# One array shape for all products but the scores: a retention layer with its feed-forward block on one core

## The chip, the cores and the metric

The kernel runs on one core of a Trainium2 chip. The metric is the device time of one execution in microseconds. The core has a TensorE (PE in the profile, its weight loads PEld), a VectorE (DVE), a ScalarE (ACT), a GpSimd (POOL) and a SyncE (SP), which here only issues DMAs. Matmuls write to PSUM; the other engines copy from there to SBUF.

## The reference, cut to what matters

```python
# q, k, v: (8 batches, 8 heads, 576 tokens, 64) float32
scores = matmul(q, k.transpose(0, 1, 3, 2)) / sqrt(64)
gamma = 1.0 - 2.0 ** (-5.0 - arange(8))                  # one decay per head
Dmat = where(rel >= 0, gamma[:, None, None] ** rel, 0.0)  # rel = query pos - key pos
attn = matmul(scores * Dmat, v)
x = attn.transpose(0, 2, 1, 3).reshape(4608, 512)
h = x @ w_in                                              # (4608, 1024)
solu = h * softmax(h)
ln = (solu - mean(solu)) / sqrt(var(solu) + 1e-6) * g_ln
out = ln @ w_out                                          # (4608, 512) float32
```

## The kernel before, in words

The 4608 tokens are taken in 36 chunks of 128. Batches go in pairs: of each pair, four chunks of 128 tokens of each batch in turn (c = 0 to 3), and then one chunk that holds the last 64 tokens of both (c = 4), four such chunks in all. The decay is taken apart into a factor on the query, one on the key or value and a state that is carried from chunk to chunk, so that inside a chunk only a triangular mask (tris) is needed. In the two-batch chunks the first 64 partitions hold one batch and the last 64 the other, and the second mask of tris cuts them apart.

Each step of a chunk is a short function with a two-letter name, and the order of all steps on all engines is written out by hand in three strings: START, LOOP (run once a chunk for 21 chunks in the middle) and END. An engine does its instructions in that order. LOOP is

```python
LOOP = """
tr:2 so:-1 tu:-2 ld:6 er:2:v m1:0 dk:0 kv:1 eu:-2:a kd:4 ad:1 cv:3:g av:1 mx:0 sc:2 sq:-2 fs:1
ex:1:a rt:-2 cq:4:g xp:0 m2:-2 d3:0 ck:5:g st:-2 mk:2
"""
```

where the number is the chunk, counted from the one in hand, and a letter names the engine (a ScalarE, v VectorE, g GpSimd). The steps that matter here:

- ld loads q, k and v of a chunk from SP's queue (L185, L192); a two-batch chunk takes two DMAs of 64 partitions for each. st scales a result on ScalarE and stores it (L523, L528).
- cq, ck and cv scale q and v (L210, L199) and cast k (L171) to 16 bits, mostly on GpSimd.
- tr and tq transpose q (and k, where a DMA does not do it) on TensorE by a product with the identity (tr L256, tp L232); er and eq copy the result to SBUF (qkT, L171).
- sc makes the scores of a head from 64 rows of the array, two heads side by side, one on the upper rows and one on the lower (L290, 64\*128 in the profile); mk masks them on VectorE (ret, L303).
- kv makes the state's new part (kp, L314) and av the masked scores times v (x, L365). Each matmul of these fills 64 columns of the array, and a pair of heads goes side by side (128\*64).
- ad adds the state on VectorE (t, L329, or L327 where a batch begins), dk and d3 scale it on GpSimd (s, L341 and L353), and fs adds the state's share to x (L380, on the whole array, 128\*128).
- ex casts x to xT; m1 is the product with w_in (h, L412; in START also L400, a row of w_in at a time), eight matmuls of 512 columns on the whole array. mx takes the maximum (nm, L422), xp the exponential (e, L428), so multiplies (u, L437).
- tu transposes u (lp, L495; in END du does it by a DMA, L500), eu copies it (uT), and m2 is the product with w_out (o, L515), again eight matmuls of 512 columns on the whole array. sq and rt make the normalisation (L465, L477 to L487).
- In END the last chunk goes in two halves of its columns (hm, hx, hp, ho, ht, he, hq, h2, hw), and hw stores each half with two DMAs, one on SP's and one on ScalarE's queue (L638).
- c1, at the start, sends for the table small (L650) and lets GpSimd make the identity and the masks.

A matmul on the profile is written rows\*columns of the array, then the output's partitions x elements. Each matmul has a weight load of its own ahead of it.

Of the kernel before, what the change touches and what calls it, by code (L numbers as in the profile page):

```python
# [10 lines left out]
FP = mybir.dt.float32  # L11
F16 = mybir.dt.float16
BF16 = mybir.dt.bfloat16
P = 128
# [55 lines left out]
def _np_tables():  # L70


    g = 1.0 - 2.0 ** (-5.0 - np.arange(H, dtype=np.float64))
    p = np.arange(P)
    gq = (g[None, :] ** p[:, None]) / 8.0
    gk = g[None, :] ** (-p[:, None])
    j = np.arange(8)
    gqt = (g[2 * (p[:, None] % 4) + j // 4] ** (4 * (p[:, None] // 4) + j % 4)) / 8.0
    gqm = (g[2 * (p[:, None] % 4) + j // 4] ** ((4 * (p[:, None] // 4) + j % 4) % 64)) / 8.0
    gkt = g[None, :] ** (-(p % 64)[:, None])  # L80


    gs = np.zeros((P, 4))
    gd = np.zeros((P, 4, 2))
    for e in range(2):
        for hp in range(4):
            gs[e * 64 : e * 64 + 64, hp] = g[2 * hp + e] ** 128.0
        gd[e * 64 : e * 64 + 64, :, e] = gs[e * 64 : e * 64 + 64]
    small = np.concatenate([gq, gk, gqt, gkt, gs, gd.reshape(P, 8), gqm], axis=1).astype(np.float32)
    return small  # L90
# [3 lines left out]
def kernel(  # L94
# [10 lines left out]
    nc = tc.nc  # L105
# [28 lines left out]

    def rows(n):

        bs, c = chunks[n]
        if c < 4:
            return [(slice(0, P), bs[0], c * P)]
        return [(slice(64 * i, 64 * i + 64), b, 4 * P) for i, b in enumerate(bs)]  # L140


    small = const.tile([P, 52], FP, name="small")
    tris = const.tile([P, 2, P], FP, name="tris")
# [14 lines left out]
    gd = small[:, 36:44].rearrange("p (a b) -> p a b", a=4)  # L159
    gqm = small[:, 44:52]  # L160

# [10 lines left out]


    def quads(n):

        return n != NCH - 2

    def ld(n):

        for key, src in (("qf", q), ("kf", k), ("vf", v)):  # L180
            dst = load.tile([P, H, D], FP, name=key, bufs=6 if key == "kf" else 7)
            for pp, b, s0 in rows(n):
                m = pp.stop - pp.start
                if key == "qf" and quads(n):
                    nc.sync.dma_start(  # L185
                        out=dst[pp].rearrange("p (h a) d -> p h (a d)", h=2),
                        in_=src[b, :, s0 : s0 + m, :].rearrange(
                            "(g h) (t a) d -> t g h (a d)", h=2, a=4
                        ),
                    )  # L190
                    continue
                nc.sync.dma_start(  # L192
                    out=dst[pp], in_=src[b, :, s0 : s0 + m, :].rearrange("h p d -> p h d")
                )
            T[key, n] = dst

# [29 lines left out]
    def tq(n):  # L226

        tp = bank([P, 2, 4, P], F16, "tp")
        for i, src in enumerate((T.pop(("q16", n)), T["k16", n])):
            s2 = src.rearrange("p h d -> p (h d)")  # L230
            for hp in range(4):
                nc.tensor.transpose(  # L232
                    out=tp[:, i, hp], in_=s2[:, hp * P : (hp + 1) * P], identity=ident
                )
        T["tp", n] = tp
# [14 lines left out]
    def tr(n):  # L250
        if chunks[n][1] == 4 or n < BY_DMA:
            return tq(n)
        tp = bank([P, 4, P], F16, "tr")
        s2 = T.pop(("q16", n)).rearrange("p h d -> p (h d)")
        for hp in range(4):
            nc.tensor.transpose(  # L256
                out=tp[:, hp], in_=s2[:, hp * P : (hp + 1) * P], identity=ident
            )
        T["tp", n] = tp
# [6 lines left out]
    def turned(engine, n, out, tp):  # L266

        if not quads(n):
            return copy(engine, out, tp)
        copy(  # L270
            engine, out.rearrange("p g (t a) -> p g t a", a=4),
            tp.rearrange("p a (t g) -> p g t a", g=4),
        )
# [98 lines left out]
    def fs(n):  # L372

        bs, c = chunks[n]
        qkT = T.pop(("qkT", n))
        s16 = [T.pop(("s16", b, c)) for b in bs] if c > 0 else []
        w = P // len(bs)
        for hp in range(4):
            for i, s in enumerate(s16):
                nc.tensor.matmul(  # L380
                    out=T["x", n][:, hp, i * w : (i + 1) * w],
                    lhsT=s[:, hp].rearrange("p e d -> p (e d)"),
                    rhs=qkT[:, 0, hp, i * w : (i + 1) * w],
                    start=False, stop=i == len(s16) - 1, skip_group_check=True,
                )
        T["xs", n] = T.pop(("x", n))
# [6 lines left out]
    def mr(n, d):  # L393

        d = int(d)
        done = T.get(("rows", n), 0)
        if done == 0:
            T["h", n] = ps_h.tile([P, DFF], FP, tag="h", name="h")
        for i in range(2):
            nc.tensor.matmul(  # L400
                out=T["h", n][:, i * 512 : (i + 1) * 512], lhsT=T["xT", n][:, d],
                rhs=w_in16[:, d, i * 512 : (i + 1) * 512], start=done == 0, stop=done == 3,
            )
        T["rows", n] = done + 1

    def m1(n):

        xT = T.pop(("xT", n))
        h = ps_h.tile([P, DFF], FP, tag="h", name="h")
        for i in range(2):  # L410
            for d in range(4):
                nc.tensor.matmul(  # L412
                    out=h[:, i * 512 : (i + 1) * 512], lhsT=xT[:, d],
                    rhs=w_in16[:, d, i * 512 : (i + 1) * 512], start=d == 0, stop=d == 3,
                )
        T["h", n] = h
# [73 lines left out]
    def tu(n):  # L490

        u = T.pop(("u", n))
        lp = bank([P, NF, P], F16, "lp")
        for c in range(NF):
            nc.tensor.transpose(out=lp[:, c], in_=u[:, c * P : (c + 1) * P], identity=ident)  # L495
        T["lp", n] = lp
# [11 lines left out]
    def m2(n):  # L508

        uT = T.pop(("uT", n))  # L510
        o = bank([P, DM], FP, "o")
        assert T["w_out"] == NF and (n < PLAIN or T["w_cen"] == NF)
        w = w_out16 if n < PLAIN else T["w_c"]
        for c in range(NF):
            nc.tensor.matmul(  # L515
                out=o, lhsT=uT[:, c], rhs=w[:, c], start=c == 0, stop=c == NF - 1
            )
        T["o", n] = o

    def st(n):  # L520

        o_sb = moe.tile([P, DM], FP, name="o_sb", bufs=4)
        nc.scalar.activation(  # L523
            out=o_sb, in_=T.pop(("o", n)), func=ACT.Copy, scale=T.pop(("rs", n))
        )
        for pp, b, s0 in rows(n):
            m = pp.stop - pp.start
            nc.sync.dma_start(out=out[b * S + s0 : b * S + s0 + m, :], in_=o_sb[pp])  # L528


    def hm(n, i):
# [5 lines left out]
        for d in range(4):  # L537
            nc.tensor.matmul(
                out=h, lhsT=T["hx", n][:, d], rhs=w_in16[:, d, i * 512 : (i + 1) * 512],
                start=d == 0, stop=d == 3,  # L540
            )
        T["hh", n, i] = h
# [40 lines left out]
    def ht(n, i):  # L583
# [3 lines left out]
        for c in range(4):  # L587
            nc.tensor.transpose(out=lp[:, c], in_=u[:, c * P : (c + 1) * P], identity=ident)
        T["hlp", n, i] = lp
# [24 lines left out]
    def h2(n, i):  # L614
# [3 lines left out]
        for c in range(NF):  # L618
            nc.tensor.matmul(
                out=o, lhsT=T["huT", n, c // 4][:, c % 4], rhs=T["w_c"][:, c, w], start=c == 0,  # L620
                stop=c == NF - 1,
            )
        T["ho", n, i] = o

    def hw(n, i, e):
# [6 lines left out]
        else:  # L632
            nc.vector.tensor_scalar(
                out=o_sb, in0=o, scalar1=rs, scalar2=None, op0=ALU.mult, op1=ALU.bypass
            )
        for queue, (pp, b, s0) in zip((nc.sync, nc.scalar), rows(n)):
            m = pp.stop - pp.start
            queue.dma_start(out=out[b * S + s0 : b * S + s0 + m, w], in_=o_sb[pp])  # L638


    def wu(_, count):

        w = bank([P, 512], FP, "w")
        for _ in range(int(count)):
            nc.tensor.matmul(
                out=w, lhsT=warm[:, 0:P], rhs=warm, start=True, stop=True, skip_group_check=True
            )

    def c1(_):
# [11 lines left out]
        )  # L661
        nc.gpsimd.memset(tris.rearrange("p a b -> p (a b)"), 1.0)
        nc.gpsimd.affine_select(
            out=tris, in_=tris, pattern=[[0, 2], [1, P]], channel_multiplier=-1, base=0,
            compare_op=ALU.is_ge, fill=0.0,
        )
        nc.gpsimd.affine_select(
            out=tris[:, 1, 64:], in_=tris[:, 1, 64:], pattern=[[0, 64]], channel_multiplier=1,
            base=-64, compare_op=ALU.is_ge, fill=0.0,
        )  # L670
# [45 lines left out]
    def mm(_):  # L716
# [3 lines left out]
        for c in range(NF):  # L720
            nc.tensor.matmul(
                out=T["mean"], lhsT=ones, rhs=w_out16[:, c], start=c == 0, stop=c == NF - 1
            )

# [53 lines left out]
```

## Time and profile before

| | us |
|---|---|
| median of 3 runs | 217.29 (215.56 to 219.33) |
| the profiled execution | 218.18 |
| its span | 216.5 |
| PE busy (matmul records) | 197.4 (91%), 1989 matmuls |
| DVE busy | 180.8 (84%) |
| POOL busy | 173.6 (80%) |
| ACT busy | 167.1 (77%) |
| DMA on SP's queue | 111904 packets, 46.55 MB, 92.7% of 16 engines' span |

The span is the time between the first and the last instruction of the profiled execution, and 1.7 us of its time lie around it. Matmuls overlap in the records: the records of a group of matmuls last longer than the distance between their starts, so a busy share of PE is not a share of its peak. The granted TensorE clock is 0.9 or more of full speed in all 40 slices of the page. DMA shares above 1 occur in single stretches, since packets of one engine overlap too.

### The profile page before, as it was taken

What the parts mean: (1) busy time and instruction counts of PE and PEld (TensorE: products, weight loads), DVE (VectorE), ACT (ScalarE), POOL (GpSimd) and SP (SyncE); (2) the same over time, 40 slices, a digit from 0 to 9 for tenths busy, and PEclk for the clock granted to TensorE, in tenths of its full rate; (3) what the DMA queues carried; (4) which work ended last, traced back from release to release, by engine and by line L of the source; (5) the groups of instructions that cost most, each with busy time, mean ns of one, the idle gap of its engine ahead of it and who ended that gap; (6) DMA issues with size and microseconds to landing.
All of it is one profiled execution on the core that took longest, in us unless ns stands there. A gap on an engine that the chain in (4) does not pass through costs nothing.

```text
span 216.5 us, 5376 instructions
## 1 busy us (share of the span) xinstructions
PE 197.4 (91%) x1989; PEld 110.8 (51%) x1989; DVE 180.8 (84%) x289; ACT 167.1 (77%) x279; POOL 173.6 (80%) x275
## 2 busy tenths in 40 slices
PE   0379889896999999999999999999999999999993
PEld 0254456453455555555555555555555565545451
DVE  1378899999997998888888898888888999889840
ACT  2073988966897888888888788888888794986991
POOL 3348889997367899999997899999997899977340
PEclk9999999999999999999999999999999999999999
DMA  5999999998986899799999998899999999674845
GB/s 137 289 317 287 228 280 358 193 245 224 270 228 168 219 183 201 177 225 258 243 223 232 255 208 186 186 247 248 214 227 213 253 181 190 145 172 100 195 109 182
DMA packets 112250, 47.04 MB, mean 217 GB/s; under 512 B 96984, under 2 KB 106208, under 8 KB 112224
## 3 DMA queue, kind: packets, MB, share of 16 engines
q1 hardware_dynamic: 111904, 46.55, 92.7%
q8 instruction: 15, 0.25, 0.5%
q10 hardware_dynamic: 320, 0.16, 0.3%
q14 instruction: 11, 0.09, 0.2%
HBM read 32.54 MB, written 9.44 MB: 194 GB/s over the span
## 4 chain that ended last, share of the span: by engine, by line
PE 78%; DVE 13%; DMA 2%; issue 2%; SPq 2%; ACT 1%; DVEq 0%; ACTq 0%
PE o L515 26%; PE h L412 23%; PE sc L290 5%; PE lp L495 5%; PE x L365 4%; PE x L380 3%; PE kp L314 3%; DVE nm L422 3%; DVE ret L303 2%; DMA vf<-in_v_dram 2%; PE tp L232 2%; PE tr L256 2%; PE h L400 2%; DVE u L437 2%; DVE q L210 1%
## 5 line engine op out<-in xcount | busy, mean ns | idle before, releaser
L412 PE MATMUL h<-w_in,xT 128*128 128x512 f16 x264 | 62.4, 379 | 0.5 <-DVE u L437 0.5
L515 PE MATMUL o<-w_c,uT 128*128 128x512 f16 x240 | 56.5, 379 | 0.6 <-DVE t L327 0.4
L428 ACT ACTIVATE e<-h,nm 128x1024 f32<-128x1024 f32 x35 | 39.0, 1116 | 14.0 <-DVE nm L422 14.0
L303 DVE TENSOR_TENSOR ret<-sc,tris 128x512 f16<-128x512 f32 x72 | 46.1, 682 | 1.3 <-PE sc L290 1.2
L437 DVE SCALAR_TENSOR_TENSOR u<-h,e 128x1024 f16<-128x1024 f32 x35 | 42.7, 1220 | 2.7 <-ACT e L428 1.4
L422 DVE TENSOR_REDUCE nm<-h 128x1 f32<-128x1024 f32 x35 | 42.5, 1216 | 2.0 <-PE h L412 1.5
L515 PEld LDWEIGHTS <-uT 128*128 128x128 f16 x280 | 26.2, 98 | 27.1 <-issue 0.4
L412 PEld LDWEIGHTS <-xT 128*128 128x128 f16 x264 | 24.2, 98 | 24.4 <-issue 0.5
L341 POOL TENSOR_TENSOR s<-t,small 128x512 f16<-128x512 f32 x32 | 34.2, 1070 | 2.6 <-DVE t L329 2.6
L199 POOL TENSOR_TENSOR v<-vf,small 128x512 f16<-128x512 f32 x32 | 33.6, 1051 | 3.0 <-DMA vf<-in_v_dram 3.0
L465 ACT ACTIVATE sq<-u,su 128x1024 bf16<-128x1024 f16 x30 | 34.8, 1159 | 0.1
L210 POOL TENSOR_TENSOR q<-qf,small 128x512 f16<-128x512 f32 x30 | 31.3, 1044 | 1.8 <-DMA qf<-in_q_dram 1.8
L171 ACT CAST xT<-x 128x512 f16<-128x512 f32 x34 | 19.9, 585 | 11.1 <-PE x L380 10.6
L523 ACT ACTIVATE o_sb<-o,rs 128x512 f32<-128x512 f32 x35 | 23.9, 685 | 4.1 <-POOL rs L487 1.6
L171 ACT COPY uT<-lp 128x1024 f16<-128x1024 f16 x25 | 25.3, 1012 | 0.3 <-PE lp L495 0.2
L487 POOL TENSOR_TENSOR rs<-w,mhalf 128x1 f32<-128x1 f32 x36 | 19.8, 551 | 3.0
L483 POOL TENSOR_SCALAR w<-ss,w 128x1 f32<-128x1 f32 x31 | 8.9, 287 | 15.9 <-ACT sq L465 13.9
L171 POOL CAST k<-kf 128x512 f16<-128x512 f32 x28 | 17.1, 611 | 3.0 <-DMA kf<-in_k_dram 3.0
L171 ACT COPY qkT<-tp 128x512 f16<-128x512 f16 x20 | 10.7, 594 | 10.9 <-PE tp L232 10.9
L495 PE MATMUL lp<-ident,u 128*128 128x128 f16 x224 | 17.0, 219 | 1.3 <-DVE u L453 1.3
L353 POOL TENSOR_TENSOR s<-t,small 128x256 f32<-128x256 f32 x24 | 14.9, 622 | 3.4 <-DVE t L327 2.5
L290 PE MATMUL sc<-qkT 64*128 64x128 f16 x288 | 15.2, 225 | 2.0 <-ACT qkT L171 1.2
(89 smaller groups left out, 262.5 us busy)
## 6 DMA issues: line engine op xcount, KB each, us to landing
qf<-in_q_dram SPq DMA_DIRECT2D x32, 256.0 KB, 4.0
kf<-in_k_dram SPq DMA_DIRECT2D x32, 256.0 KB, 4.4
vf<-in_v_dram SPq DMA_DIRECT2D x32, 256.0 KB, 4.7
out_dram<-o_sb SPq DMA_DIRECT2D x32, 256.0 KB, 2.6
w_in<-in_moe_w_in_dram SPq DMA_DIRECT2D x4, 512.0 KB, 6.1
w_out<-in_moe_w_out_dram SPq DMA_DIRECT2D x4, 512.0 KB, 6.7
qf<-in_q_dram SPq DMA_DIRECT2D x8, 128.0 KB, 3.2
kf<-in_k_dram SPq DMA_DIRECT2D x8, 128.0 KB, 3.8
```

The lines of the kernel that those rows point to most:

```text
L171: (engine.copy if engine is nc.scalar else engine.tensor_copy)(out=out, in_=in_)
L199: engine.tensor_tensor(out=dst, in0=T.pop((key, n)), in1=table.unsqueeze(2).to_broadcast([P, H, D]), op=ALU.mult,)
L210: ENG[e].tensor_tensor(out=dst.rearrange("p (a h) d -> p h a d", h=2), in0=T.pop(("qf", n)).rearrange("p (h a) d -> p h a d", h=2), in1=ta ...
L303: nc.vector.tensor_tensor(out=r, in0=s, in1=m, op=ALU.mult)
L341: nc.gpsimd.tensor_tensor(out=s16, in0=t.unsqueeze(2).to_broadcast([P, 4, 2, D]), in1=gd.unsqueeze(3).to_broadcast([P, 4, 2, D]), op=ALU.mult,
L412: nc.tensor.matmul(out=h[:, i * 512 : (i + 1) * 512], lhsT=xT[:, d], rhs=w_in16[:, d, i * 512 : (i + 1) * 512], start=d == 0, stop=d == 3,)
L422: nc.vector.tensor_reduce(out=nm, in_=T["h", n], axis=AX.X, op=ALU.max, negate=True)
L428: nc.scalar.activation(out=e, in_=T["h", n], func=ACT.Exp, bias=T.pop(("nm", n)), accum_out=s)
L437: nc.vector.scalar_tensor_tensor(out=u, in0=T.pop(("h", n)), scalar=-1.0, in1=T.pop(("e", n)), op0=ALU.mult, op1=ALU.mult, accum_out=su,)
L465: nc.scalar.activation(out=s, in_=T.pop(("v", n)), func=ACT.Square, scale=-float(DFF), bias=T.pop(("su", n)), accum_out=ss,)
L495: nc.tensor.transpose(out=lp[:, c], in_=u[:, c * P : (c + 1) * P], identity=ident)
L515: nc.tensor.matmul(out=o, lhsT=uT[:, c], rhs=w[:, c], start=c == 0, stop=c == NF - 1)
```

## The change

All products and transposes on the whole array become two matmuls, each on 64 columns of the array, that write the lower and the upper 64 partitions of the same output (product and turn). Those that were on 64 columns (kv, av) or on 64 rows (sc) stay. The order of the steps and the PSUM banks stay too.

The two-batch chunks hold the two batches' tokens in turn (partition 2t is token t of the first, 2t + 1 of the second), and are loaded with one DMA for each of q, k and v, and stored with one. For that the tables of decays of these chunks, the second mask, the copy of the transposed q and the reads of fs are laid out anew. GpSimd makes the second mask as a product of the first with par, two new columns of small.

```diff
+    def tokens(src, n):
+        bs, c = chunks[n]
+        if c < 4:
+            return src[bs[0], :, c * P : (c + 1) * P, :].rearrange("h t d -> t h d")
+        return src[bs[0] : bs[1] + 1, :, 4 * P :, :].rearrange("b h t d -> t b h d")
...
+    HALF = (slice(0, 64), slice(64, P))
+    def turn(out, in_):
+        for w in HALF:
+            nc.tensor.transpose(out=out[w], in_=in_[:, w], identity=ident)
+    def product(out, lhsT, rhs, start, stop):
+        for w in HALF:
+            nc.tensor.matmul(
+                out=out[w], lhsT=lhsT[:, w], rhs=rhs, start=start, stop=stop,
+                skip_group_check=True,
+            )
...
@@ ld @@
-            for pp, b, s0 in rows(n):
-                m = pp.stop - pp.start
...
+                nc.sync.dma_start(out=dst, in_=tokens(src, n))
...
@@ tq, tr, tu, ht @@
-                nc.tensor.transpose(
-                    out=tp[:, i, hp], in_=s2[:, hp * P : (hp + 1) * P], identity=ident
-                )
+                turn(tp[:, i, hp], s2[:, hp * P : (hp + 1) * P])
...
@@ turned, two-batch chunks @@
+            engine, out.rearrange("p g (t a b) -> p g t a b", a=4, b=2),
+            tp.rearrange("p a (t b g) -> p g t a b", b=2, g=4),
...
@@ fs @@
+        def part(t, i):
+            return t if len(bs) == 1 else t.rearrange("p (t b) -> p b t", b=2)[:, i]
         for hp in range(4):
             for i, s in enumerate(s16):
-                nc.tensor.matmul(
-                    out=T["x", n][:, hp, i * w : (i + 1) * w],
-                    lhsT=s[:, hp].rearrange("p e d -> p (e d)"),
-                    rhs=qkT[:, 0, hp, i * w : (i + 1) * w],
-                    start=False, stop=i == len(s16) - 1, skip_group_check=True,
+                product(
+                    part(T["x", n][:, hp], i), s[:, hp].rearrange("p e d -> p (e d)"),
+                    part(qkT[:, 0, hp], i), False, i == len(s16) - 1,
                 )
...
@@ m1; mr, m2, hm, h2, mm and wu likewise @@
-                nc.tensor.matmul(
-                    out=h[:, i * 512 : (i + 1) * 512], lhsT=xT[:, d],
-                    rhs=w_in16[:, d, i * 512 : (i + 1) * 512], start=d == 0, stop=d == 3,
-                )
+                w = slice(i * 512, (i + 1) * 512)
+                product(h[:, w], xT[:, d], w_in16[:, d, w], d == 0, d == 3)
...
@@ st, two-batch chunks @@
+            nc.sync.dma_start(
+                out=dst[:, 4 * P :, :].rearrange("b t m -> t b m"), in_=o_sb
+            )
...
@@ c1 @@
-        nc.gpsimd.affine_select(
-            out=tris[:, 1, 64:], in_=tris[:, 1, 64:], pattern=[[0, 64]], channel_multiplier=1,
-            base=-64, compare_op=ALU.is_ge, fill=0.0,
+        m = tris[:, 1].rearrange("p (t b) -> p t b", b=2)
+        nc.gpsimd.tensor_tensor(
+            out=m, in0=tris[:, 0].rearrange("p (t b) -> p t b", b=2),
+            in1=par.unsqueeze(1).to_broadcast([P, 64, 2]), op=ALU.mult,
         )
```

TensorE has 3145 matmuls after the change and 1989 before it; the instructions of the other engines stay the same in number and order, but for SP's DMAs of the two-batch chunks (three for a load and one for a store, before six and two) and GpSimd's masks in c1.

## The prediction

> **What bounds the kernel now.** I read the page first: the shares of the engines, then the chain that ended last.
>
> ```profile
> span 216.5 us, 5376 instructions
> PE 197.4 (91%) x1989; PEld 110.8 (51%) x1989; DVE 180.8 (84%) x289; ACT 167.1 (77%) x279; POOL 173.6 (80%) x275
> ...
> PE 78%; DVE 13%; DMA 2%; issue 2%; SPq 2%; ACT 1%; DVEq 0%; ACTq 0%
> ```
>
> TensorE is 91% busy and makes up 78% of the chain. The table by stretches of 10 us shows it all but gapless from 60 to 210 us (9.6 to 10.0 busy), while three of the four stretches from 20 to 60 hold only 8.1 to 8.8. So what counts is how closely its groups follow each other. The timeline of PE alone shows that for one round of LOOP; columns are start, time to the end of the last, and the instructions.
>
> ```profile
> 102.33 0.39 PE L232 MATMUL tp<-ident,k 128*128 128x128 f16 x4
> 102.55 0.61 PE L495 MATMUL lp<-ident,u 128*128 128x128 f16 x8
> 103.00 1.89 PE L412 MATMUL h<-w_in,xT 128*128 128x512 f16 x8
> 104.82 0.32 PE L314 MATMUL kp<-v,k 128*64 128x64 f16 x8
> 104.96 0.39 PE L365 MATMUL x<-ret,v 128*64 128x128 f16 x8
> 105.29 0.40 PE L290 MATMUL sc<-qkT 64*128 64x128 f16 x8
> 105.62 0.40 PE L380 MATMUL x<-qkT,s 128*128 128x128 f16 x4
> 105.85 0.38 PE L515 MATMUL o<-w_c,uT 128*128 128x512 f16 x1
> ```
>
> Read starts, not durations, since matmuls overlap. Eight lp matmuls of 128 columns take 102.55 to 103.00, 56 ns each. Eight h matmuls of 512 columns start 216 ns apart, so the next group could start at 104.73; it starts at 104.82. The single records say it exactly: 309 ns from the last h matmul to the first kp, where 216 stand between h matmuls: 93 ns are lost. The same loss stands at x L365 to sc (about 96) and sc to x L380 (92), and none stands at tp to lp, lp to h or L380 to o. What the three places share is a change in the part of the array used: 128\*128, 128\*64 (a column half), 64\*128 (a row half). Over the trace I find 119 such changes between these three shapes; where nothing else is late, each costs 92 to 96 ns. The pair after the first is late too: 52 ns after kp's first instead of 31.
>
> The list of waits shows the same from the side of the weight loads:
>
> ```profile
> PEld L314 <- issue: 9.1, 22, 0.6
> ...
> PEld L365 <- issue: 2.9, 8, 0.4
> PEld L290 <- issue: 2.9, 7, 0.4
> ```
>
> Loads otherwise run ahead of the matmuls; at these lines, the first of a new shape, they sit idle for about 0.4 us and wait for nothing that the profile names.
>
> **The change, part by part.** *Shapes.* turn and product split every matmul on the whole array into two on its column halves. The whole-array shape is then gone (but for gT), and only changes to and from sc are left: 22 from column to row, 13 from whole to row, 32 and 3 back stay as 35 pairs of changes; 34 from whole to column and 15 back vanish, 49 in all. From 57 to 168 us there are 23 of the 49, none with a wait in it: 23 x 93 ns = 2.1 us, and the late second pair, 23 x 21 ns = 0.5 us. After 168 us there are 10 without a wait, 1.1 us with their second pairs; PE waits there now and then for ACT and DVE, so I take 0.7. Before 57 us there are 10, 1.2 us; PE waits there for loads and casts, and I take 0.5. Against it, the pair after the first is 11 ns late when sc gives way to the whole array and 21 ns when h gives way to a column half: 35 x 10 ns = 0.4 us lost. Sum 3.4 us.
>
> *Twice the matmuls.* 580 of 512 columns, 16 of 256, 432 transposes and 128 of x L380 become 1156 more, with as many loads. A pair costs nothing if its halves run side by side. The rows for that are x L365 and kp, which are such pairs already: the halves start 3 to 4 ns apart, and pairs start 56 ns apart at 128 columns and 28 to 29 at 64, as one whole-array matmul would. For 512 columns with one moving operand for both halves no row exists. Bounds: 0 from x L365; above, the one burst where the halves were 16 to 19 ns apart (sc at 185.97 us), 580 x 17 = 9.9 us if it added to every pair. I take 0, as the 56 ns row repeats in every chunk and moves as many columns per ns.
>
> The row of the loads is x L365 again: two loads of 64 columns begin 3 ns apart, and the pair still takes 56 ns. The Trainium skill (TensorEngine Tiling (Array Packing), Restrictions and Gotchas) says that column tiling goes without fast weight load, and (TensorE: Matmul & The Clock Gate, LDWEIGHTS (loading the stationary operand)) that an ordinary load takes its columns over 1.2 ns. As an estimate from these pages, two loads one after the other would be 107 ns, and 432 transposes would lose 51 ns each, 22 us; by that rule the change is a plain loss (a rival below). The trace speaks against it: x L365 lives without the fast load at 56 ns per pair.
>
> *Issue.* A chunk of LOOP has 56 matmuls and 56 loads now (tr 4, tu 8, m1 8, kv, av, sc 8 each, fs 4, m2 8), and 88 of each after: 176 instructions in 5.25 - 0.11 = 5.14 us, 29 ns each. The trace shows 47 ns sustained (5.25 us / 112), which is no limit found, and one burst that is: at 185.86 us PE's sequencer stands in an event wait before sc, and the 16 instructions behind it begin between 185.95 and 186.15, 13 ns each. I take 13, so 0.
>
> *Two-batch chunks.* Four of 36 chunks: loads go from six DMAs of 128 KB to three of 256, stores from two to one (the last chunk keeps two each for its halves). Bytes and pieces stay.
>
> ```profile
> qf<-in_q_dram SPq DMA_DIRECT2D x32, 256.0 KB, 4.0
> kf<-in_k_dram SPq DMA_DIRECT2D x32, 256.0 KB, 4.4
> ...
> kf<-in_k_dram SPq DMA_DIRECT2D x8, 128.0 KB, 3.8
> ```
>
> One large landing at 4.4 us replaces two small at 3.8, issued 0.6 apart: the same time. SP saves three issues of 0.6 us per chunk, which nobody waits for, as loads come one to three chunks ahead. Copies of q and x L380 take elements in steps of two for these chunks; DVE stands idle some 0.5 us a chunk before t L329, which hides 0.1 or 0.2 us, and 8 pairs of 29 ns in each of four chunks could at worst double on PE, 0.9 us. I take 0.1. POOL's new product in tris needs small, which landed 1.6 us after its issue at 0.80; POOL then has 2.71 us of idle time before k L171: 0.
>
> *What follows PE.* A faster PE must be fed. POOL repeats its round of LOOP in 5.39 us while PE needs 5.25:
>
> ```profile
> 87.71 1.04 POOL L341 TENSOR_TENSOR s<-t,small 128x512 f16<-128x512 f32 x1
> ...
> 93.10 1.04 POOL L341 TENSOR_TENSOR s<-t,small 128x512 f16<-128x512 f32 x1
> ...
> 98.50 1.04 POOL L341 TENSOR_TENSOR s<-t,small 128x512 f16<-128x512 f32 x1
> ```
>
> Its s (dk) is what x L380 waits for. In the trace s is ready 1.17 us ahead at the start of such a stretch (chunk at 76.5 us) and 0.61 ahead at 97.5; then come chunks with less for POOL, and the lead returns. With 0.11 us less per chunk the smallest lead is about 0.61 - 5 x 0.11 = 0.05, in the second stretch 0.69 - 0.55 = 0.14. It just holds; I take 0.1 us for it.
>
> Sum: -3.4 + 0.1 + 0.1 = -3.2 us. The profiled execution took 218.18 us (span 216.5 and 1.7 around it), which makes 215.0. The median of the runs shown is 217.29, 0.9 below it; from there, 214.1. I say 214.0.
>
> **The rivals.** *All of it counts:* the waits in the first 57 and last 45 us follow PE, since PE's own results end them. Then the sum is 2.6 + 1.1 + 1.2 - 0.4 = 4.5 us, 212.8. For it: DVE and ACT there wait for tp, x and h. Against: DMA and POOL do too.
>
> *POOL takes the place of the shape changes:* its lead runs out and PE falls into POOL's 5.39 us. For it, the falling lead above; against, POOL's idle time of 14.7 us between 60 and 180. If the lead is gone halfway, half of the loop's 2.6 us goes: 215.4; if all is lost, 217.
>
> *Slower, issue becomes the bound:* 176 instructions a chunk decide as soon as one takes over 29 ns on the average. The nearest sustained row: after the event wait at 109.93 us, 32 instructions up to 110.96 at 30.5 ns each, at the array's own pace there. If that is the limit, a chunk takes 5.37 us, 0.12 more than now, over 30 chunks 3.6 us: 220.9. Against it, the 13 ns burst. The Trainium skill (TensorE: Matmul & The Clock Gate, Step-by-step: what each phase is for) knows a case of about 62 ns per matmul; 88 of them would be 5.46 us a chunk and 6 us more in all. kp's eight matmuls start within 0.12 us, so the trace does not show that, though a queue filled ahead could hide it.
>
> *Slower, pairs of 512 columns do not overlap fully:* from 6 ns per pair (3.4 us / 580) the gain is gone; at 17 ns it is 217.3 - 3.2 + 9.9 = 224.0. The loads belong here too: if the halves of a transposed pair went one after the other, at 56 ns each, 432 x 56 ns = 24 us would come on top, against the row of x L365; of the 0.07 below I give that 0.02.
>
> *The change does not do what it says:* the 93 ns belong to the tensors, not the shape. Against it, groups of one shape but other tensors (tp to lp, lp to h, x L380 to o) follow at the array's own pace. 217.
>
> **How the numbers follow.** My forecast 0.62, all of it counts 0.12, POOL 0.08, no effect 0.03, issue 0.08, pairs 0.07. The runs of before spread over 215.56 to 219.33, so my own case reaches from 211.6 to 216.4. The range 211.0 to 219.5 takes it, the two rivals without effect and the near edge of the slower ones. Faster by over 2% (below 212.9; 2% is about what a measurement of this kernel can tell from no change): a third of my case and two thirds of the next, 0.30. Slower by over 2%: both slower rivals and a rest, 0.17. Within: 0.53.
>
> **What would show it.** Right: kp starts 216 ns after the last pair of h, the PEld waits on issue at kp gone, h pairs 216 ns apart, a LOOP round near 5.14 us, waits of x L380 on POOL under 0.5 us in all. Wrong: pairs of h over 222 ns apart, gaps inside lp or x after an event wait, or PE idle in front of x L380 or sc.

## The result, and the profile after

The first measurement gave 216.35 us median for the changed kernel (214.59 to 221.44, 21 runs) beside 218.08 for the kernel before (215.56 to 219.44, 21 runs): a ratio of 0.9928, with a 95% interval of 0.9899 to 0.9958. The same kernel was measured twice more: 217.96 beside 218.09 (ratio 1.0052, 1.0004 to 1.0099) and 218.43 beside 218.82 (1.0004, 0.9958 to 1.0050). Over all 41 runs of the changed kernel the median is 217.97 us, over the 73 of before in the same three measurements 218.29. So the forecast's sign and range (211.0 to 219.5) stood in the first measurement, at half the forecast gain of 3.2 us, and the repeats leave 0.3 us, which is no difference that these runs can tell from none. The intervals of the first two measurements do not meet, so from one measurement to the next more differs than an interval shows; what it is stays open. (The ratios leave disturbed runs out; the medians take all runs.)

The page of the first profile after, engines and chain:

```profile
span 214.6 us, 7661 instructions
PE 194.8 (91%) x3145; PEld 127.9 (60%) x3145; DVE 178.2 (83%) x289; ACT 166.6 (78%) x279; POOL 173.6 (81%) x275
...
PE 45%; POOL 16%; DMA 13%; DVE 10%; SPq 5%; ACT 5%; issue 4%; POOLq 0%; DVEq 0%; ACTq 0%
```

TensorE's share of the chain falls from 78% to 45%; POOL, DMA and SP's queue come in. TensorE's own groups follow as forecast. Their timeline for a round of LOOP (start, time to the end of the last, instructions):

```profile
78.69 1.68 PE L196 MATMUL h<-w_in,xT 128*64 128x512 f16 x14
80.20 0.29 PE L335 MATMUL kp<-v,k 128*64 128x64 f16 x8
80.32 0.39 PE L386 MATMUL x<-ret,v 128*64 128x128 f16 x8
80.65 0.40 PE L311 MATMUL sc<-qkT 64*128 64x128 f16 x8
80.98 0.41 PE L196 MATMUL x<-qkT,s 128*64 128x128 f16 x8
81.22 1.89 PE L196 MATMUL o<-w_c,uT 128*64 128x512 f16 x16
```

The seven pairs of h shown take 78.69 to 80.20, 216 ns each, and kp follows the last pair at that distance, where it took 309 ns before. The halves of a pair start 3 to 4 ns apart, 128-column pairs 56 ns apart. h starts at 78.47, 83.62, 88.77 and 93.91 us: a round of 5.14 to 5.15, against 5.25. Between the three shapes 70 changes are left of 119, all to or from sc. In the list of the weight loads' waits, kp's line (L335 now) falls from 9.1 us, 22 times, to one wait; the lines of sc and of the pairs' transposes keep 3.3 and 2.4 us:

```profile
PEld L335 <- issue: 0.9, 1, 0.9
```

The loads of the two-batch chunks are single ones now. The k transposes land later than before, in the median 4.9 us after their issue (end of the line) and not 4.2:

```profile
qkT<-k SPq DMA_TRANSPOSE x21, 4.9
```

One group is slower by the change. In the two-batch chunks the matmuls of x L380 (L196 now) read q and write x in steps of two. Before, with the new layout alone (an experiment below) and after, the groups of chunk 17:

```profile
110.75 0.41 PE L380 MATMUL x<-qkT,s 128*128 128x64 f16 x8
```

```profile
111.04 0.62 PE L196 MATMUL x<-qkT,s 128*128 128x64 f16 x8
```

```profile
106.81 0.64 PE L196 MATMUL x<-qkT,s 128*64 128x64 f16 x16
```

The next group starts 0.24, 0.43 and 0.44 us after these. The single records say why: the matmuls of 64 columns start 29 ns apart before, 56 with the steps of two. That is 0.2 us in each two-batch chunk, 0.9 us in the four of the first profile (the last, in END, takes 0.51 beside 0.23).

What became of the change is seen when the same groups are found in four profiles (start in us, and distance to the kernel before):

| TensorE group | before | after, 1st | after, 2nd | after, 3rd |
|---|---|---|---|---|
| tp, early in LOOP | 65.15 | 62.16 (-2.99) | 63.37 (-1.78) | 65.56 (+0.41) |
| sc of chunk 23 | 136.78 | 132.19 (-4.59) | 133.40 (-3.38) | 135.59 (-1.19) |
| sc of chunk 30 | 172.16 | 167.80 (-4.36) | 171.58 (-0.58) | 173.41 (+1.25) |
| lph, near the end | 206.95 | 205.14 (-1.81) | 209.12 (+2.17) | 210.24 (+3.29) |
| span | 216.5 | 214.6 | 218.6 | 219.7 |

From the first row to the second every profile of the changed kernel gains the same 1.6 us: fourteen rounds of 0.11 us (the change of shapes) and a wait of 0.4 us for t at 121.58 us that only the kernel before has there, less what chunk 17 takes more. Ahead of it START decides, anywhere from 3 us early to 0.4 late. Behind it all three lose: 2.8, 5.6 and 4.5 us between the second row and the fourth. The first profile's execution took 216.31 us, near the median of its measurement; the second's and third's took 220.30 and 221.38 us, 2.3 and 3.0 above the medians of theirs, so they show what a large loss is made of, not its usual size. The lists of TensorE's waits from 57 us on (total, times, longest), before, then after in the first and in the third profile:

```profile
PE o L515 <- DVE t L327: 0.4, 1, 0.4
PE tr L256 <- DVE qkT L171: 0.2, 1, 0.2
```

```profile
PE tr L191 <- ACT o_sb L539: 0.9, 1, 0.9
PE o L196 <- DMA uT<-u: 0.6, 1, 0.6
PE x L196 <- POOL s L362: 0.5, 1, 0.5
PE sc L311 <- DVE qkT L183: 0.5, 1, 0.5
PE sc L311 <- DMA qkT<-k: 0.4, 1, 0.4
...
```

```profile
PE sc L311 <- DMA qkT<-k: 2.7, 2, 1.4
PE tr L191 <- ACT o_sb L539: 0.9, 1, 0.9
PE x L196 <- POOL s L362: 0.4, 1, 0.4
...
```

The scores now wait for the k that a DMA transposes: 0.4 us in the first profile, 3.0 in the second, 2.7 in the third. In the first profile, of the first measurement, four other waits are longer.

### The profile page after: what moved, and what is told of

Read it like the earlier page. It is cut to its first block, busy times and chain, and to the rows that moved or that the text cites. A ratio compares the mean times of both kernels' runs of the same rounds, so it can differ in the third digit from the quotient of the medians.

```text
span 214.6 us, 7661 instructions
## 1 busy us (share of the span) xinstructions
PE 194.8 (91%) x3145; PEld 127.9 (60%) x3145; DVE 178.2 (83%) x289; ACT 166.6 (78%) x279; POOL 173.6 (81%) x275
## 4 chain that ended last, share of the span: by engine, by line
PE 45%; POOL 16%; DMA 13%; DVE 10%; SPq 5%; ACT 5%; issue 4%; POOLq 0%; DVEq 0%; ACTq 0%
PE o L196 16%; PE h L196 15%; DMA kf<-in_k_dram 4%; POOL s L362 3%; PE lp L191 3%; POOL v L219 3%; DMA vf<-in_v_dram 3%; DMA qkT<-k 3%; PE sc L311 2%; PE x L196 2%; DMA qf<-in_q_dram 2%; DMA uT<-u 2%; DVE nm L440 2%; SPq L210 2%; POOL q L230 2%
## 5 line engine op out<-in xcount | busy, mean ns | idle before, releaser
L196 PE MATMUL h<-w_in,xT 128*64 128x512 f16 x560 | 67.4, 381 | 0.5 <-DVE w_in L183 0.3
L196 PE MATMUL o<-w_c,uT 128*64 128x512 f16 x480 | 57.2, 380 | 0.8 <-DMA uT<-u 0.6
L196 PEld LDWEIGHTS <-xT 128*64 128x64 f16 x576 | 32.7, 110 | 21.9 <-issue 1.0
L196 PEld LDWEIGHTS <-uT 128*64 128x64 f16 x560 | 32.4, 110 | 22.3 <-DMA uT<-u 1.1
L183 ACT CAST xT<-x 128x512 f16<-128x512 f32 x34 | 19.9, 586 | 10.3 <-PE x L196 10.0
L501 POOL TENSOR_SCALAR w<-ss,w 128x1 f32<-128x1 f32 x31 | 8.3, 267 | 13.3 <-ACT sq L483 11.1
L191 PEld LDWEIGHTS <-q 128*64 128x64 f16 x280 | 12.5, 114 | 9.0 <-issue 2.4
L191 PE MATMUL lp<-ident,u 128*64 128x128 f16 x448 | 17.1, 219 | 0.6 <-DVE u L471 0.6
```

What stands on the lines that cost most here:

```text
L183: (engine.copy if engine is nc.scalar else engine.tensor_copy)(out=out, in_=in_)
L191: nc.tensor.transpose(out=out[w], in_=in_[:, w], identity=ident)
L196: nc.tensor.matmul(out=out[w], lhsT=lhsT[:, w], rhs=rhs, start=start, stop=stop, skip_group_check=True,)
```

## The experiments

**Which half of the change does what.** Pairs alone, in the old layout with six loads and two stores for a two-batch chunk (run twice):

```diff
 kernel before, and:
+    HALF = (slice(0, 64), slice(64, P))
+    def turn ...  def product ...      (as in the change, at all the same places)
```

> The kernel before with all whole-array products and transposes as column pairs, and the two-batch chunks as they were (two DMAs of 64 partitions each). Theory A (the gain is the shape changes, and the last 50 us give part of it back because the last loads and transposes by DMA do not come sooner): the same as the whole change, ratio to before 0.993 (0.990 to 0.996). Rival B (the new layout with one DMA of 256 KB a load is what costs at the end, 4.96 us landing of the last q): without it the gain is whole, 0.985 to 0.988.

> The pairs without the new layout, once more, for a trace at the full clock. Theory A (the pairs gain in the middle, and the end, fed by DMA through SP's queue, gives it back): a round of the middle at 5.14 us as in the whole change, and the excess of 4 to 5 us over the whole change stands after 160 us, where the last two-batch chunk's six loads and two stores hold up the transposes behind them on SP. Rival E (pairs with the old layout lose in the middle, by a mechanism of the array): a round over 5.25 us.

Layout alone, which is the changed kernel with whole-array products:

```diff
-    HALF = (slice(0, 64), slice(64, P))
+    HALF = (slice(0, P),)
```

> The changed kernel with whole-array products and transposes again, so the new layout of the two-batch chunks alone. Theory A: 1.000 (0.997 to 1.003), a round of the middle 5.25 us as before. Rival B: 1.004 to 1.008, slower by the time the last loads land later. Rival C (the fewer DMAs are what gained, the pairs nothing): 0.993.

Pairs alone are slower: ratio to before 1.0156 (1.0095 to 1.0216), again 1.0162 (1.0057 to 1.0266). Layout alone: 1.0036 (1.0000 to 1.0072). Neither half gains, and together they come out better than pairs alone by 1.0 to 2.3%. So an edit that I had put at 0.1 us decides whether the other one costs time. The loss of layout alone is about what x L380 takes more in four chunks (0.19 us each, 0.35% in all). Pairs alone met none of the cases: the round is 5.14 us, but the losses begin before 160 us, with a wait of 1.6 us at 141.46. The waits of pairs alone (second run) say where:

```profile
PE sc L301 <- DMA qkT<-k: 3.3, 3, 1.6
PE x L184 <- POOL s L352: 1.3, 1, 1.3
```

**Is a change of shape worth what I said?** The changed kernel with tu's transposes on the whole array, two more changes in a chunk that has them:

```diff
-            turn(lp[:, c], u[:, c * P : (c + 1) * P])
+            nc.tensor.transpose(out=lp[:, c], in_=u[:, c * P : (c + 1) * P], identity=ident)
```

> The changed kernel with the transposes of u (tu, 28 of 36 chunks) on the whole array again: two changes of shape more in each of 28 chunks. Theory A: each costs 93 ns and up to 20 for the second pair, so a round of the middle takes 5.14 + 0.2 = 5.35 us and the 21 rounds 4 us more; the ratio to before is 1.005 to 1.015. If the changes of shape are not what costs, 0.993 and 5.14 us.

1.0071 (1.0017 to 1.0125). Over 20 rounds (57 to 163 us) TensorE fell 4.14 us behind the first profile after: 0.21 a round, 0.10 per change. The price holds. But from there to the end this kernel got 2.9 us back, as its waits after 57 us were down to this one:

```profile
PE tr L191 <- DVE qkT L183: 0.2, 1, 0.2
```

The slower TensorE meets no other waits there; the faster one runs into the pace of what feeds it. (The ratio alone would hardly show the price: the changed kernel's own three measurements reach from 0.9928 to 1.0052.)

**Does the end hang on SP's queue?** In both kernels, one load in END moved forward in SP's order:

```diff
-... ld:-1 ad:-6 ...   ... d3:-6 ld:0 mx:-6 ...
+... ld:-1 ld:0 ad:-6 ...   ... d3:-6 mx:-6 ...
```

> The changed kernel with the load of the last chunk issued straight behind that of the chunk before it, ahead of two DMA transposes in SP's order (buffers are free by then). Theory A, if the last q and k are late because they are issued late: q of the last chunk lands 3 us sooner, the end gives 1 to 2 us, 0.985 to 0.989. Rival D (the DMA engines are full, 98% of the span, and what is issued sooner only pushes others back): 0.993, with transposes landing later instead.

> The kernel before with the same early load. Theory A: TensorE is the chain there to the end, so 1.000 (0.998 to 1.002). If it gains as much as in the changed kernel (0.993 or less), the late load was a loss of both kernels and not what took the change's gain.

The changed kernel: 1.0081 (1.0034 to 1.0128), with sc waiting 2.5 us for k. The kernel before: 1.0021 (0.9981 to 1.0061), with 0.2 us. Nothing is gained. Of the 2.5 us, 1.6 come at chunk 30, whose transpose is issued ahead of the moved load, and 0.9 at chunk 33, whose transpose stands behind it in SP's queue.

**Are the DMA engines full?** Both kernels store only 128 of 512 columns of the chunks from 20 on (c < 4); the other columns of those outputs are not written:

```diff
-            nc.sync.dma_start(out=dst[0, c * P : (c + 1) * P, :], in_=o_sb)
+            w = slice(0, 128 if n >= 20 else DM)
+            nc.sync.dma_start(out=dst[0, c * P : (c + 1) * P, w], in_=o_sb[:, w])
```

> The changed kernel, where chunks from 20 on store 128 of 512 columns (the rest of their output is left out; two-batch chunks store all), 192 KB less of about 1.2 MB by DMA per chunk. Theory A with full DMA engines: transposes and last loads land sooner, TensorE's waits after 160 us (2 to 3 us) mostly go, 0.980 to 0.985. If the end hangs on the order in SP's queue or on GpSimd and not on the engines of the DMA: no change, 0.992.

> The kernel before with the same light stores (the rest of that output is left out). Theory A: TensorE sets the end there and waits for nothing, so 0.998 to 1.002. If it gains as much as the changed kernel does, DMA bound both kernels alike.

0.9963 (0.9906 to 1.0020) and 1.0004 (0.9952 to 1.0057): 192 KB less per chunk brought nothing that shows, and in the changed kernel sc still waits 1.8 us for k. It is not the bytes of the late part.

**Is it the number of DMAs that SP issues?** The changed kernel, with only the two-batch DMAs cut in two again:

```diff
 ld, two-batch chunks (st likewise):
+                m = part.shape[0] // 2
+                for i, w in enumerate(HALF):
+                    nc.sync.dma_start(out=view[w], in_=part[i * m : (i + 1) * m])
```

> The changed kernel with its own layout, copies and pairs; only the single DMAs of the four two-batch chunks are cut in two again, one for partitions 0 to 63 and one for 64 to 127 (six loads, two stores). Theory: it is the time that SP spends on issuing (about 6.0 us for such a chunk's loads and stores against 2.5) that makes the k transposes late once TensorE's round is 5.14 us. Then sc waits for qkT<-k by DMA 1 to 3 us in all, above all behind the two-batch chunk near 132 us, and the ratio to before is 1.003 to 1.016, most of the way to the pairs in the old layout (1.016). Rival: the order of the tokens and the copies that go with it are what helps, not the number of issues; then no such wait, and 0.990 to 0.996 as the change itself.

> The changed kernel with the two-batch DMAs cut in two, once more, for a second profile. Theory (SP's issuing makes the k transposes late): if TensorE is on time at the start, sc near 137 us and later waits 1 to 3 us for qkT<-k by DMA. Rival (the loss lies in START): the groups are late by 2 us or more before 57 us again, and LOOP and END lose under 0.5 us.

1.0119 (1.0069 to 1.0170), again 1.0120 (1.0025 to 1.0215): three quarters of the loss of pairs alone, with layout and pairs untouched. The first profile was 6 us behind the first one of the changed kernel already in START and showed just 0.7 us of waits for k, so by itself it spoke for the rival; the second shows 2.7 us of them. Hence two kernels that split only later chunks (17, 26, 35) or only the first (8):

> The changed kernel with the two-batch DMAs of chunks 17, 26 and 35 cut in two, and chunk 8 (in START) left whole. If the loss of 1.9% from single to split DMAs comes from the k transposes in LOOP and END, this kernel has most of it, ratio to before 1.003 to 1.012; if it comes from START, 0.990 to 0.997.

> The changed kernel with only the DMAs of chunk 8 (in START) cut in two. If the loss comes from START, ratio to before 1.003 to 1.012, with TensorE's groups 2 us or more later by 57 us; if it comes from LOOP and END, 0.990 to 0.997.

Later chunks: 1.0034 (0.9973 to 1.0095), from four of its twelve runs; the median of all is 221.01 us beside 218.09. First: 0.9995 (0.9950 to 1.0039), median 217.77. By ratio the first case is only just in the band of the theory, and the two do not add up to the 1.2% of all four; the waits are clear. Later chunks split, then first chunk split:

```profile
PE sc L314 <- DMA qkT<-k: 4.3, 3, 1.9
```

```profile
PE sc L314 <- DMA qkT<-k: 0.7, 1, 0.7
```

SP's timeline around chunk 17's store and chunk 26's loads, first in the changed kernel (third run), then with later chunks split:

```profile
133.25 0.61 SPq L547 DMA_DIRECT2D out_dram<-o_sb  x1
133.90 0.59 SPq L210 DMA_DIRECT2D qf<-in_q_dram  x1
134.54 0.62 SPq L214 DMA_DIRECT2D kf<-in_k_dram  x1
135.20 0.67 SPq L214 DMA_DIRECT2D vf<-in_v_dram  x1
136.04 1.83 SPq L259 DMA_TRANSPOSE qkT<-k  x1
```

```profile
132.29 1.25 SPq L556 DMA_DIRECT2D out_dram<-o_sb  x2
133.59 1.34 SPq L217 DMA_DIRECT2D qf<-in_q_dram  x2
134.98 1.31 SPq L217 DMA_DIRECT2D kf<-in_k_dram  x2
136.33 2.54 SPq L217 DMA_DIRECT2D vf<-in_v_dram  x2
139.04 1.23 SPq L262 DMA_TRANSPOSE qkT<-k  x1
```

The four steps take 2.8 us, or 6.8 when each is two DMAs, and the k transpose of chunk 24 stands behind them in the same queue. SP issues one thing after the other with under 0.2 us between. The scores that need that k, in the same two kernels:

```profile
142.22 0.40 PE L311 MATMUL sc<-qkT 64*128 64x128 f16 x8 [1.42 <-DMA qkT<-k]
```

```profile
142.00 0.40 PE L314 MATMUL sc<-qkT 64*128 64x128 f16 x8 [1.95 <-DMA qkT<-k]
```

So the quantity to watch is the lead: the time from SP's issue of a chunk's k transpose to the start of the scores that use it (waits included). From these two views of each profile, in us:

| chunk | before | after, 1st | after, 3rd | later split | LOOP stores on ScalarE |
|---|---|---|---|---|---|
| 12 | 10.2 | 9.1 | 9.7 | 9.7 | 9.7 |
| 18 | 8.6 | 8.9 | 8.9 | 8.1 | 10.3 |
| 19 | 9.2 | 6.7 | 5.9 | 6.4 | 9.8 |
| 24 | 7.1 | 5.5 | 6.2 | 3.0 | 12.2 |
| 25 | 7.4 | 5.4 | 5.8 | 4.1 | 12.0 |
| 30 | 7.0 | 5.4 | 5.5 | 5.9 | 10.6 |

The transposes land 4.9 us (median) after their issue, so the lead is gone near 5. From chunk 18 to 25 SP's issues of k are 5.4 us apart in the kernel before and 5.7 after (38.0 and 39.6 us for seven), TensorE's rounds 5.25 and 5.14. The lead shrinks with the difference. (With the light stores above it is 6.2 and 5.8 us at chunks 24 and 25, as in the changed kernel: fewer bytes do not keep it.) Why SP is slower after the change, with fewer DMAs to issue, stays open: the issue of one k transpose lasts 1.2 to 4.1 us in these profiles.

**Taking the stores off SP.** In the chunks of END, in LOOP, or for every second chunk, issued from ScalarE's queue instead:

```diff
+        queue = nc.scalar if n >= 26 else nc.sync                   # END
+        queue = nc.scalar if 9 < n < 26 else nc.sync                # LOOP
+        queue = nc.scalar if n > 9 and n % 2 == 0 else nc.sync      # every second
-            nc.sync.dma_start(out=dst[0, ...
+            queue.dma_start(out=dst[0, ...
```

> The changed kernel with the stores of the chunks from 26 on (nine of them in END) issued from ScalarE's queue, behind the activation that makes their data, in place of SP's. Theory: what the end gives back hangs on SP's issuing, 0.5 to 0.6 us per store. Then TensorE's waits for uT and qkT by DMA in the last 55 us (1.0 us) go, and the kernel gains 0.5 to 1.5 us on the change: ratio to before 0.985 to 0.991. Rival: ScalarE, which TensorE waits for 0.9 us at tr, gets later by its own issues; then 0.993 to 1.002, with a longer wait of tr for o_sb.

> The changed kernel with the stores of chunks 10 to 25 (LOOP) issued from ScalarE's queue in place of SP's: SP has some 0.6 us less to issue per chunk of 5.14 us. Theory (SP's pace in LOOP eats up the lead of the k transposes): the time from issue to sc stays at 7.5 us or more at chunks 24 and 25 (5.4 in the changed kernel), TensorE's waits for qkT<-k by DMA in the last 80 us go to under 0.5 us, and the kernel is 0.3 to 1.5% faster than the changed kernel in the same call. Rival: the DMA engines, not SP's issuing, set the pace; then the lead falls to 6 us or less all the same. Second rival: ScalarE, which has about 0.7 us of idle time per round, becomes late by its issues of 0.4 us, and LOOP's round grows above 5.2 us.

> The changed kernel with the stores of the even chunks from 10 to the last whole one issued from ScalarE's queue: SP has 0.3 us per chunk less, ScalarE 0.2 more. Theory (SP's pace): the lead at chunks 24 and 25 is 6.5 to 8 us, waits for qkT<-k under 1 us, ratio 0.2 to 1% below the changed kernel in the same call. Rival (DMA engines): lead and ratio as in the changed kernel.

END: 1.0054 (1.0011 to 1.0096). LOOP: 1.0190 (1.0120 to 1.0261). Every second: 1.0032 (0.9982 to 1.0083), beside 1.0004 of the changed kernel on the same chip. None is faster. With the stores of END moved, sc still waits 1.3 us for k, since the lead is nearly used up before END (6.0 us at chunk 25), and tr waits 0.4 us for o_sb, less than the 0.9 us of the first profile after; neither case was met. Every second store moved, the lead at chunks 24 and 25 is 6.5 and 7.5 us, in the theory's band, but one wait of 1.1 us is left (the theory had under 1) and no gain that these runs can tell. There SP spent part of the time that it saved on longer transposes: from 57 to 170 us an issue takes 2.7 us in the median, in the three profiles of the changed kernel 2.1 to 2.5. The LOOP kernel shows the mechanism in its chunks 12 to 19: with 0.6 us less to issue per chunk, the same bytes moved and TensorE at nearly the same pace (36.8 us from sc of chunk 12 to that of 19, 36.4 in the changed kernel), the lead holds at 8.8 to 10.3 us, where the changed kernel has 5.9 to 7.6 left at chunk 19. So it is SP's queue that uses up the lead there, not the bytes. Its later leads show less, since TensorE itself is then late: no sc waits for k by DMA any more, but one waits 3.4 us for uT. Waits of TensorE, and ScalarE's own timeline:

```profile
PE sc L311 <- ACT uT L183: 4.6, 3, 3.4
```

```profile
111.08 0.69 ACT L539 ACTIVATE o_sb<-o,rs 128x512 f32<-128x512 f32 x1
115.85 0.34 ACTq L546 DMA_DIRECT2D out_dram<-o_sb  x1
116.23 1.01 ACT L183 COPY uT<-lp 128x1024 f16<-128x1024 f16 x1 [4.46 <-DMA qkT<-k]
```

A store on ScalarE's queue stood 4.1 us until a k transpose issued by SP at 109.27 had landed, with uT behind it. The trace's records show what held it: the instruction ahead of the store waits for the semaphore on which that transpose counts its landing, and the store counts its own on the same one. So it is the program's ordering and not ScalarE's time for issuing (0.34 us), and the second rival is right in the loss, not in its cause.

**START.** Two more profiles of the changed kernel, and one of it with GpSimd's k of chunk 8 and s of chunk 5 put where VectorE makes w_c:

```diff
-... cq:8:v ws:3:v rt:0 xp:3 tu:4 ex:6:a ws:7:v ld:10 ws:4:v ck:8:g dk:5 st:1 ...
+... cq:8:v ck:8:g dk:5 ws:3:v rt:0 xp:3 tu:4 ex:6:a ws:7:v ld:10 ws:4:v st:1 ...
```

> The changed kernel once more, for a second profile. If START's gain belongs to the kernel, TensorE's groups up to 57 us stand within 0.5 us of where the first profile had them, and 3 us or more ahead of the kernel before. If it belongs to the execution, they may stand 1 to 2.5 us later, and VectorE's w_c then take 0.6 to 1.1 us each in place of 0.36.

> The changed kernel a third time, in five rounds. If the gain of the first measurement (0.9928) is the kernel's, the ratio to before is 0.990 to 0.996; if the two measurements are draws from the same spread of executions, 0.994 to 1.003.

> The changed kernel with one place of START moved: GpSimd makes k of chunk 8 and s of chunk 5 (0.61 and 1.04 us) directly before, not after, its small operations for rs of chunk 0, so that they run beside VectorE's three w_c in a row. Theory: VectorE and GpSimd slow each other when such operations meet, and that the change missed this meeting by chance is most of what it won in the first 57 us. Then the three w_c take 2 to 3 us in place of 1.09, tp and h behind them come 1 to 2.4 us later by 50 us, and the ratio to before is 0.995 to 1.005. Rival: the gain there comes from the shape changes; then the w_c stay at 0.4 us each, TensorE's groups stay where they are within 0.3 us, and the ratio is 0.990 to 0.996.

The gain before 57 us belongs to the execution: in the third profile of the changed kernel the operations that were slow in the kernel before are slow again. VectorE by shape, up to 57 us (busy, mean ns, idle before), before and in the first profile after:

```profile
L210 DVE TENSOR_TENSOR q<-qf,small 128x512 f16<-128x512 f32 x4 | 4.4, 1112 | 4.4 <-DMA qf<-in_q_dram 4.4
...
L706 DVE TENSOR_SCALAR w_out<-w_out,g 128x512 f16<-128x512 f32 x1 | 1.3, 1294 | 0.0
```

```profile
L230 DVE TENSOR_TENSOR q<-qf,small 128x512 f16<-128x512 f32 x4 | 2.8, 689 | 3.9 <-DMA qf<-in_q_dram 3.9
...
L723 DVE TENSOR_SCALAR w_out<-w_out,g 128x512 f16<-128x512 f32 x1 | 0.5, 476 | 0.0
```

The third profile has q at 1111 and w_out at 1281 ns. With the moved GpSimd work, q, s and w_c meet and all are slower:

```profile
46.05 1.08 DVE L230 TENSOR_TENSOR q<-qf,small 128x512 f16<-128x512 f32 x1
46.55 1.48 POOL L362 TENSOR_TENSOR s<-t,small 128x512 f16<-128x512 f32 x1
47.05 1.93 DVE L745 TENSOR_TENSOR w_c<-w_out,warm 128x512 f16<-128x512 f16 x3
```

In the first profile after, q took 0.69, s 1.04 and the three w_c 1.09. That they slow each other is thus shown; the time is not (0.9968, 0.9893 to 1.0042), since TensorE was already 1.9 us late at 37.7 us, ahead of the moved steps. What makes them meet in one execution and not in another stays open.

## Why the prediction was right or wrong

*Loop: right.* Shape changes cost what the gaps said, the second pair came in time, the round is 5.14 us as worked out, in three profiles alike.

*Issue and pairs at 0: right.* 176 instructions go through in 5.14 us, and pairs of 512 columns stay 216 ns apart. Neither of these slower rivals occurred. Nor did the one in which the 93 ns belong to the tensors and not to the shape.

*POOL's lead: right.* s is 0.95 us ahead at the start of a stretch, falls to about 0 and recovers; x waits 0.5 and 0.4 us once in the first and third profile, and not in the second.

*Two-batch chunks at 0.1: too small.* The case named as the worst, x L380 at twice its time (0.9 us), is what came.

*What follows PE, put at 0.1 for POOL and at nothing for SP's queue: the step that failed.* Its reason stands under the two-batch chunks: "SP saves three issues of 0.6 us per chunk, which nobody waits for". For POOL I worked out how a lead shrinks when TensorE's round does. For SP I did not, though the same traces held it: the lead of the k transposes is 5.7 us at chunk 15 and 7.1 at chunk 24, 7.0 to 9.8 between, landing after 4.2. I looked at loads, which come one to three chunks ahead, and not at the k transpose that queues behind them. The saving is four issues (three loads and a store), 4.0 us in the two views above. With the pairs, somebody does wait, and the saved issues are worth 0.7 to 1.9%, by the kernels with all of them cut in two. The Trainium skill (DMA: Bandwidth & Descriptors, Issuing engines are not separate DMA queues) says that issuing from several engines saves only the sequencer's time, usually small beside the transfer. The LOOP kernel above agrees with the first half; here that time was not small, since without it the lead held up to chunk 19.

*The end at 0.7 gained: wrong in sign.* From chunk 23 on the profiles lose 2.8 to 5.6 us. Faster rounds in LOOP are given back here: a kernel 0.21 us a round slower got 2.9 us back. In the second and third profile sc's waits for k are 3.0 of 5.6 and 2.7 of 4.5 us. In the first they are 0.4 of 2.8; beside x L380's two-batch chunks the rest is waits for o_sb, uT, s and qkT, which no experiment takes apart. So for the execution in the middle of the first measurement the cause is shown only in part: what feeds TensorE came too late, and SP's queue is the one feeder that the experiments single out.

*Start at 0.5 gained: not measurable.* Between the executions it moves by 3.4 us, with VectorE and GpSimd meeting or not. One profiled execution of before was taken as its START; a second profile would have shown how far it moves.

*The sum.* 1.6 won in LOOP, 3 won to 0.4 lost in START by chance, 2.8 to 5.6 lost at the end: spans of 214.6, 218.6 and 219.7 against 216.5. That the first profile is ahead at all is luck: without START's 3 us it would be behind. (The spread of the runs of before, put around 214.0, is 212.3 to 216.0, not 211.6 to 216.4; nothing hangs on it.) The slower rivals were all about TensorE's own pairs or issue. The one that came, a feeder's queue in front of sc, was named only in the last line ("PE idle in front of x L380 or sc").

## What to carry to other kernels

Before a gain on the bounding engine is booked, work out the lead of every feeder, DMA queues included: time from issue to use, minus landing time, and how much it shrinks per round. A queue that issues without idle time is as full as an engine, although the busy table does not list it, and an edit that thins it can be worth nothing alone and yet decide whether another edit costs. Look at what a new layout does to the steps in which the matmuls read and write. Compare a stage's time over more than one execution: here LOOP repeated to 0.1 us and START did not to 3.

## What the runs showed of the hardware

A wait of TensorE can cost more than its length. In the second profile after, sc waited 2.41 us, and the next groups ran at about half pace:

```profile
171.58 0.56 PE L311 MATMUL sc<-qkT 64*128 64x128 f16 x8 [2.41 <-DMA qkT<-k]
172.07 3.39 PE L196 MATMUL h<-w_in,xT 128*64 128x512 f16 x16
```

h takes 1.92 us elsewhere. In the table by stretches of 5 us the last three figures are the granted clock, the DMA share and GB/s; the clock is 0.67 here and 0.99 to 1.00 in the stretches beside it:

```profile
170.00:175.00 5.00, 3.42 (x22) 1.55 (x24) 2.47 (x5) 2.17 (x4) 3.79 (x6) 0.67 1.08 239
```

After 1.64 us of waiting in the kernel with the early load h took 3.59. But the length of the wait does not decide it alone: after waits of 1.54 us (second kernel with split DMAs), 1.59 (pairs alone), 1.95 (later chunks split, at 142.00) and 2.32 us (moved GpSimd work) the next group of 512 columns took 1.89 to 1.92 us as always. One execution of pairs alone ran at a granted clock of 0.65 from 50 us on and took 290.96 us.

Matmuls of 64 columns that read and write every second element start 56 ns apart, twice the 29 of those without steps. Which of the two, the reading or the writing, costs it these runs do not tell.

VectorE operations and GpSimd operations that meet slow each other by up to a factor of 2.7 (w_out 476 to 1294 ns, q 689 to 1112). The Trainium skill (SBUF — State Buffer, Who interferes with whom) says that a VectorE instruction with two SBUF inputs contends with a GpSimd instruction that reads SBUF; q and w_c, which have two, agree. w_out, with one tensor input, is slowed too, which that sentence does not cover.
